# Fetches of the second pass held to set times, new planner durations, and one weight pair converted beside the last chunk's value products

## The chip, the cores and the metric

The kernel runs on one core of one Trainium2 chip. A core has TensorE (PE: matmuls, and their weight loads, shown as PEld), VectorE (DVE), ScalarE (ACT), GpSimd (POOL) and SyncE (SP), which here only issues DMAs. The metric is the device time of one execution in microseconds (us), lower is better.

## The reference

Three layers follow each other on a batch of 4 sequences of 576 tokens and 512 features, all in fp32. Attention is windowed: heads 0 to 3 look at the last 32 tokens, heads 4 to 7 at every fourth of the last 128.

```python
scores = scale * q @ k.T                      # masked per head to its window
x = softmax(scores) @ v                       # -> [4, 576, 512]

x_prev = shift of x by one token
xk = mu_k * x + (1 - mu_k) * x_prev
xr = mu_r * x + (1 - mu_r) * x_prev
k = maximum(xk @ w_k, 0)                      # 512 -> 1024
x = sigmoid(xr @ w_r) * (k * k @ w_v)         # 1024 -> 512

h = maximum(x.T @ w_tok1, 0) @ w_tok2         # over the tokens: 576 -> 256 -> 576
u = x + h.T
h2 = maximum(u @ w_ch1, 0) @ w_ch2            # 512 -> 1536 -> 512
out = u + h2
```

## The kernel before

**Arithmetic.** A product of fp32 values is made of three matmuls on split operands: each operand is kept as a high and a low part (two fp32r values), and high*high, high*low and low*high are added in PSUM. So each weight and each activation has to be converted first: ACT usually makes the high part (a copy with rounding) and DVE the low part (a subtraction). The two large channel products (`w_ch1`, `w_ch2`) go by a scheme with seven products of half blocks in place of eight, named A11, S1, A12, S2, S4, S3 and A22; for it, sums and differences of blocks of weights and activations are formed on DVE as well.

**Stages.** In the order of the program:

- attention, 36 units; the later ones lie beside the second layer;
- the second layer, in chunks of columns: `keys` (products with `w_k`), `mix` (products with `w_v`, here "value products"; they gather in the PSUM banks 68 to 70, and DVE frees a bank with a multiplication, `x<-x,bank`, before the next chunk's value products can use it) and `receptance` (products with `w_r`). The loop over `g` holds chunks 0 to 3, and the last chunk, chunk 5, comes behind it in a loop over `n` (`mixes(5, n)`);
- the third layer over tokens (a loop over `b`, the four sequences), then the first channel product, then the second one. The second channel product is called the second pass here: `result(c)` for c = 0, 1, 2, each for a third of the tokens.

**Weights converted early.** The weights of the channel products are converted while the second layer runs. `weight_1(j)` does pair j of column blocks of `w_ch1`: it loads two blocks, forms four sums, splits seven blocks into high and low parts and writes them to DRAM (`part_w`). `weight_ks(j)` makes sums of `w_k` blocks (`part_k`), `weight_2(j)` does a pair of `w_ch2` (`part_A`, `part_S`). The tables `W1_AT`, `K_AT` and `W2_LATE` say at which step g, or how early in the token stage, each one stands. They work in the tiles `raw`, `wv` and `x` (or, with the places called `amid`, in `xt` and `wk`).

**The second pass.** The first channel product's outputs are kept in DRAM (`part_mid`, three arrays of 8 pieces of 128x1152, 576 KB each), and so is u (`part_u`). `result(c)` loads its pieces with `load(q)`, q = 0 to 3 being the four quarters (two pieces each), and its part of u in two DMAs. Then it goes through seven sweeps of 36 matmuls each, A11, S1, A12, S2, S4, S3, A22. Between the sweeps DVE adds u or a sum to what a sweep left in PSUM (`plus`, in the trace `z<-bank,...` and `y<-bank,...`) and `send` writes 128x384 pieces of 192 KB to the output (`outT<-z`, `outT<-y`). The pieces to be sent lie in a ring of three places of two pieces each (`two(out_r)`: tiles named z, z and y), so that an addition into a place has to wait until that place's send before has landed. The sweep A22 goes on in the banks of S3, so that it can start only when DVE has read those banks.

**Order.** All instructions are first recorded by the class `Plan`, with the engines that may run each. `Plan.order` then plays the program with a duration for each instruction (`_cost`) and sets the order on each engine: of what is ready, the instruction with the earliest due time goes next. Due times come from the place of the TensorE work that needs a result. `hold` keeps an instruction from starting before its place in the program (the sum of TensorE time ahead of it) plus a number of us; `floor` makes conversions that were recorded through `slowly` due no earlier than 20 us behind their place, and sets their hold to 0; `SPARE` is time added behind a load that a conversion needs. Nothing of this is done on the chip: what is left there is one fixed order per engine, with semaphores between them. All instructions are issued from one line (L421), so the profile's groups are told apart by tile.

Of the kernel before, what the change touches and what calls it, by code (L numbers as in the profile page):

```python
# [19 lines left out]
C = H * D  # L20
# [33 lines left out]
TILES = [sum(n for _, _, n in c) // 128 for c in CHUNKS]  # L54
FIRST = [sum(TILES[:c]) for c in range(len(CHUNKS))]
N2 = 384
W1_AT, K_AT, W2_LATE, SLACK = (8, 11, 13, 16, 18, 21), (9, 12, 16, 19), (4, 7, 10, 13), 20.0
NAMES = "A11", "S1", "A12", "S2", "S4", "S3", "A22"
NEG = -1.0e30
MASKED = 1  # L60
# [94 lines left out]
class Plan:  # L155
# [17 lines left out]
    }  # L173
    TAIL = dict(tensor=0.0, vector=0.08, scalar=0.10, gpsimd=0.0, sync=0.0)
    TICK, BUSY = 10.24 / 3, 3060
    SPARE = 3.0

    def __init__(self, nc):
        self.nc = nc
# [77 lines left out]
    @staticmethod  # L257
    def _cost(engine, method, kw):

        out = kw["out"]  # L260
        cols = int(np.prod(out.shape[1:]))
        pointers = sum(hasattr(kw.get(k), "space") for k in ("scale", "bias", "scalar", "scalar1"))
        if engine == "sync":
            if kw["in_"].dtype == U32:
                return max(0.45, 4 * cols * out.shape[0] / 230e3 - 0.9)
            return max(0.45, 8 * (0.03 + 4 * cols * 0.0266e-3))
        if engine == "tensor":
            if kw.get("is_transpose"):
                return cols / 1200 + 0.0025
            if kw["lhsT"].dtype in (F32R, BF16):  # L270
                return cols / 2263 + 0.0049
            if kw["lhsT"].shape[0] <= D or out.shape[0] <= D:
                return cols / 1200 + 0.0025
            return 2 * max(cols / 1200 + 0.0025, 0.112)
        source = kw.get("in_", kw.get("in0"))
        psum = source is not None and "PSUM" in str(source.space)
        if engine == "scalar":
            read = 0.093 * (kw.get("accum_out") is not None)
            return (0.07 if psum else 0.1) + cols / 1200 + 0.03 * pointers + read
        if engine == "gpsimd":  # L280
            return 0.04 if method == "memset" else 0.04 + cols / 345
        if method == "tensor_reduce":
            return 0.066 + int(np.prod(source.shape[1:])) / 960
        if method == "reciprocal":
            return 0.066 + cols / 157
        fast = method in ("tensor_copy", "tensor_scalar", "tensor_scalar_add") and not psum
        return 0.066 + 0.05 * pointers + cols / (1920 if fast else 960)

    def _run(self, at, cost, kw):

# [144 lines left out]
def tile_model(nc, banks, kept_k, kept_1, kept_w, kept_u, kept_mid, units, cst, mu, w_k, w_v, w_r, w_t1, w_t2, w_c1, w_c2, outT):  # L435
# [21 lines left out]
    def ring(*places):  # L457
        return Ring(at, sum((p if isinstance(p, list) else [p] for p in places), []))
# [47 lines left out]
    def col_block(w, m, n=128):  # L506

        return words(w).rearrange("(k p) c -> p k c", p=128)[:, :, 2 * n * m:2 * n * m + 2 * n]
# [290 lines left out]
    def quarters(j, load, order, raws, fresh, both=both, sums=sums):  # L799

        for i in range(2):
            single([(everything, load(j + 6 * i))], both[:, i].flat(), raws)
        a11, a12, a21, a22 = (both[:, k // 2, k % 2] for k in order)
        combine(sums[:, 0], a21, a22, ALU.add)
        combine(sums[:, 1], sums[:, 0], a11, ALU.subtract)
        combine(sums[:, 2], a11, a21, ALU.subtract)
        combine(sums[:, 3], a12, sums[:, 1], ALU.subtract)
        for name, v in zip(NAMES, (a11, sums[:, 0], a12, sums[:, 1], sums[:, 3], sums[:, 2], a22)):
            t = fresh.tile(2, 256, dtype=F32R)
            split(v, t[:, 0], t[:, 1])  # L810
            yield name, f(t)

    def weight_1(j):
        for n, (_, t) in enumerate(quarters(j, lambda m: col_block(w_c1, m), (0, 1, 2, 3), raw_c, fresh)):
            nc.sync.dma_start(out=kept_1[j][:, n], in_=t)

    def weight_ks(j):
# [18 lines left out]
    def slowly(convert, *args):  # L836
        start = len(nc.ops)
        convert(*args)
        nc.floor.update(dict.fromkeys(range(start, len(nc.ops)), SLACK))
        nc.hold.update(dict.fromkeys(range(start, len(nc.ops)), 0.0))  # L840
# [3 lines left out]
    for g in range(8 * nchunk + 2):  # L844
        c, m = divmod(g, 8)
        kr = 2 if c else 0
        if g == 0:
            k_ring = psum(3)
        elif g == 10:
            k_ring, s_ring = psum(3, 4), psum(0)  # L850
        if m == 0 and c < nchunk:
            for which in range(2):
                for kt in KT:
                    prep(c, which, kt)
        if g >= 2:
            cv, mv = divmod(g - 2, 8)
            if cv == 0 and mv % 2 == 0:
                weight_v(mv // 2)
            for j in range(TILES[cv]):
                mix(cv, mv, j)  # L860
        if c == 0 and m % 2 == 0:
            weight_k(m // 2)
        if c < nchunk:
            keys(c, m, k_ring)
        if g in W1_AT:
            slowly(weight_1, W1_AT.index(g))
        if g in K_AT:
            slowly(weight_ks, K_AT.index(g))
        for h in beside.get(2 * g, []):
            attend(h, s_ring, t_ring, x_ring)  # L870
        if c < nchunk and kr <= m < kr + TILES[c]:
            if c == 0 and m == kr:
                for kt in range(4):
                    weight_r(kt)
            receptance(c, m - kr, k_ring)
        for h in beside.get(2 * g + 1, []):
            attend(h, s_ring, t_ring, x_ring)
# [95 lines left out]
    def mixes(c, n, first=5):  # L973
        m = order_m[n]
        h, l = (k2_r.tile(N2, dtype=F32R) for _ in range(2))
        split(k2[c, m], h, l)
        for j in range(TILES[c]):
            if n == 0:
                vp[j] = bank(first + j, (C,))
            mm3(vp[j], h[:, rows(j)], l[:, rows(j)], *wv[m], n == 0, n == 7)  # L980
            if n == 7:
                t = x2[FIRST[c] + j]
                nc.vector.scalar_tensor_tensor(out=t, in0=t, scalar=1.0, in1=vp[j], op0=ALU.add, op1=ALU.mult)
# [22 lines left out]
    receptance(4, 1, k_ring)  # L1006
    receptance(4, 2, k_ring)
    mixes(4, 7)
    for n in range(8):
        mixes(5, n)  # L1010
        if n % 2 == 0 and n < 6:
            receptance(5, n // 2, k_ring)

# [157 lines left out]
            r = rest[:, kt, 64 * (b % 2):64 * (b % 2) + 64].split(2, 32)  # L1171
            nc.vector.tensor_tensor(out=t, in0=r, in1=t, op=ALU.add)

    amid = ring(cut("xt", (2,), 2 * C)), ring(cut("wk", (2,), 512)), at(("wk", 3, 0), (2, 2, 256)), at(("wk", 3, 1024), (4, 256))
    for b in range(B):
        if b < 6 - len(W2_LATE):
            slowly(weight_2, b, *amid)
        tokens_in(b)
        if b == 2:
            for j in (1, 2):  # L1180
                fetch_1(j)
        if b:
            tokens_out(b - 1)
# [92 lines left out]
    def result(c):  # L1276
# [43 lines left out]

        x, y, z = two(x_r), two(y_r), two(z_r)
        on = dict(first=False, goes_on=True)
        load(0)
        load(1)
        for kt in range(4):
            nc.sync.dma_start(out=us[kt], in_=kept_u[c][:, kt])
        load(2)
        load(3)
        sweep("A11", parts(0), x)
        s1 = two(aside_r)  # L1330
        plus(x, u_of(0, 0), s1)
# [117 lines left out]
```

## Time and profile before

| | |
|---|---|
| device time, median of 3 runs | 673.16 us (673.02 to 673.44) |
| the profiled execution | 671.81 us |
| its span in the trace | 670.0 us |
| PE busy | 653.8 us, 98% |
| DVE, ACT, POOL busy | 566.7 (85%), 371.4 (55%), 2.1 us |
| TensorE's granted clock | 1.00 throughout (the 2.4 GHz level) |
| moved by DMA | 146.45 MB |

The profiled execution took 1.81 us more than its span, and was 1.35 us shorter than the median of the runs. Busy time is the share in which an engine executes; an engine's idle time is put down to whatever released it.

### The profile page before, as it was taken

What the parts mean: (1) busy time and instruction counts of PE and PEld (TensorE: products, weight loads), DVE (VectorE), ACT (ScalarE), POOL (GpSimd) and SP (SyncE); (2) the same over time, 40 slices, a digit from 0 to 9 for tenths busy, and PEclk for the clock granted to TensorE, in tenths of its full rate; (3) what the DMA queues carried; (4) which work ended last, traced back from release to release, by engine and by line L of the source; (5) the groups of instructions that cost most, each with busy time, mean ns of one, the idle gap of its engine ahead of it and who ended that gap; (6) DMA issues with size and microseconds to landing.
All of it is one profiled execution on the core that took longest, in us unless ns stands there. A gap on an engine that the chain in (4) does not pass through costs nothing.

```text
span 670.0 us, 11558 instructions
## 1 busy us (share of the span) xinstructions
PE 653.8 (98%) x4105; PEld 603.0 (90%) x4105; DVE 566.7 (85%) x1188; ACT 371.4 (55%) x981; POOL 2.1 (0%) x22
## 2 busy tenths in 40 slices
PE   6899999999999999999999999999999999899997
PEld 6678888888888888998889899999999999899997
DVE  4999998799799989777699888798898569899982
ACT  4989785789669875435278555264474122312310
POOL 0000000000000000000000000000000000000000
PEclk9999999999999999999999999999999999999999
DMA  8989444675774535713533769777697999933211
GB/s 325 385 310 331 142 126 150 190 261 166 249 237 149 198 115 179 237 38 121 164 111 133 233 193 364 275 254 256 247 356 253 413 408 412 392 107 95 71 36 59
DMA packets 65385, 146.45 MB, mean 219 GB/s; under 512 B 5808, under 2 KB 24368, under 8 KB 64304
## 3 DMA queue, kind: packets, MB, share of 16 engines
q1 hardware_dynamic: 65328, 145.72, 62.3%
q8 instruction: 32, 0.52, 0.3%
q14 instruction: 25, 0.20, 0.1%
HBM read 95.89 MB, written 49.81 MB: 217 GB/s over the span
## 4 chain that ended last, share of the span: by engine, by line
PE 72%; DVE 11%; DMA 9%; ACT 5%; issue 1%; SPq 0%; DVEq 0%; ACTq 0%
PE bank L421 72%; DVE z L421 3%; DVE at L421 2%; DVE x L421 2%; DMA z<-part_mid 2%; ACT z L421 2%; DVE wv L421 1%; ACT at L421 1%; ACT x L421 1%; DMA outT<-z 1%; DMA outT<-y 1%; DMA x<-w_k 1%; DMA wr<-units 1%; DMA part_mid<-at 1%; DMA at<-units 1%
## 5 line engine op out<-in xcount | busy, mean ns | idle before, releaser
L421 PE MATMUL bank<-z,wk 128*128 128x384 f32 x644 | 141.9, 345 | 0.3 <-ACT z L421 0.3
L421 PE MATMUL bank<-wv,z 128*128 128x512 f32 x432 | 124.3, 402 | 1.3 <-ACT raw L421 1.3
L421 PEld LDWEIGHTS bank<-z,wk 128*128 128x128 f32 x644 | 112.7, 188 | 5.7 <-ACT z L421 0.9
L421 PEld LDWEIGHTS bank<-wv,z 128*128 128x128 f32 x432 | 78.0, 188 | 14.6 <-ACT raw L421 1.6
L421 ACT ACTIVATE at<-at 128x96 f32<-128x96 f32 (+3 forms) x183 | 67.0, 369 | 36.3 <-DVE at L421 34.9
L421 ACT ACTIVATE z<-z 128x384 fp32r<-128x384 f32 (+1 forms) x90 | 46.4, 523 | 23.2 <-DVE z L421 15.7
L421 PE MATMUL bank<-xt,wk 128*128 128x384 f32 x254 | 54.0, 346 | 0.8 <-ACT at L421 0.8
L421 PE MATMUL bank<-wr,z 128*128 128x512 f32 x192 | 53.7, 406 | 1.0 <-DVE z L421 1.0
L421 PE MATMUL bank<-xt,x 128*128 128x384 f32 x248 | 48.8, 334 | 0.0
L421 PE MATMUL bank<-z,x 128*128 128x384 f32 x232 | 47.0, 334 | 0.0
L421 PEld LDWEIGHTS bank<-xt,wk 128*128 128x128 f32 x254 | 44.4, 188 | 2.6 <-issue 1.1
L421 DVE TENSOR_TENSOR z<-z,z 128x384 fp32r<-128x384 f32 (+1 forms) x78 | 44.2, 574 | 1.8 <-ACT z L421 0.6
L421 PEld LDWEIGHTS bank<-xt,x 128*128 128x128 f32 x248 | 43.5, 188 | 0.0
L421 DVE TENSOR_TENSOR at<-bank,at 128x384 f32<-128x384 f32 x64 | 35.2, 552 | 7.8 <-PE bank L421 7.2
L421 PEld LDWEIGHTS bank<-wr,z 128*128 128x128 f32 x192 | 34.3, 188 | 7.3 <-DVE z L421 1.3
L421 PEld LDWEIGHTS bank<-z,x 128*128 128x128 f32 x232 | 40.8, 188 | 0.0
L421 ACT ACTIVATE x<-bank 96x512 f32<-96x512 f32 (+1 forms) x48 | 28.1, 589 | 11.8 <-PE bank L421 11.6
L421 ACT ACTIVATE at<-bank 128x384 f32<-128x384 f32 x36 | 17.5, 488 | 27.0 <-PE bank L421 26.2
L421 DVE TENSOR_TENSOR raw<-raw 128x256 f32<-128x256 f32 (+1 forms) x76 | 30.2, 420 | 0.2
L421 PE MATMUL bank<-at 128*128 128x96 f32 (+1 forms) x121 | 22.1, 275 | 5.4 <-DMA at<-cst 5.0
L421 PE MATMUL bank<-cst,at 128*96 128x128 f32 x144 | 26.8, 274 | 0.2 <-DVE at L421 0.2
L421 PE MATMUL bank<-z,at 128*128 128x512 f32 x96 | 25.5, 397 | 0.0
(234 smaller groups left out, 1327.1 us busy)
## 6 DMA issues: line engine op xcount, KB each, us to landing
part_mid<-at SPq DMA_DIRECT2D x18, 768.0 KB, 5.9
z<-part_mid SPq DMA_DIRECT2D x11, 576.0 KB, 9.3
x<-w_c SPq DMA_DIRECT2D x12, 512.0 KB, 4.0
at<-units SPq DMA_DIRECT2D x14, 416.0 KB, 3.7
unit<-units SPq DMA_DIRECT2D x13, 416.0 KB, 3.8
at<-units SPq DMA_DIRECT2D x21, 256.0 KB, 3.4
part_w<-wv SPq DMA_DIRECT2D x21, 256.0 KB, 2.7
part_w<-x SPq DMA_DIRECT2D x21, 256.0 KB, 3.0
```

The costliest lines, as they stand in the source:

```text
L421: call(kw["out"], kw["constant"]) if method == "memset" else call(**kw)
```

## The change

- In `result(c)` the loads have the same order in the program as before (quarters 0 and 1, then u, then quarters 2 and 3), but for c = 1 and 2 each group now has a hold: -5, -5, 0, +5, +5 us against its place. Before they had none.
- In `_cost` the durations that the planner assumes for DMAs, ACT and DVE become longer; `SPARE` becomes 2 instead of 3.
- `W1_AT` has five steps instead of six. The sixth pair of `w_ch1` is now recorded in the last chunk, behind `mixes(5, 2)`, in the places `amid`.
- `weight_2(0)` is recorded behind `mixes(5, 5)` (before: at sequence 0 of the token stage), `weight_2(1)` at sequence 2 (before: at sequence 1). `K_AT` has later steps.

The number of instructions of each kind stays: what is computed is the same.

```diff
-W1_AT, K_AT, W2_LATE, SLACK = (8, 11, 13, 16, 18, 21), (9, 12, 16, 19), (4, 7, 10, 13), 20.0
+W1_AT, K_AT, W2_LATE, SLACK = (8,12,16,19,22), (10,14,18,21), (4,7,10,13), 20.0
...
-    SPARE = 3.0
+    SPARE = 2.0
...
-            return max(0.45, 8 * (0.03 + 4 * cols * 0.0266e-3))
+            return max(0.45, 8 * (0.045 + 4 * cols * 0.0266e-3))
...
-            return (0.07 if psum else 0.1) + cols / 1200 + 0.03 * pointers + read
+            return (0.08 if psum else 0.11) + cols / 1170 + 0.03 * pointers + read
...
-        return 0.066 + 0.05 * pointers + cols / (1920 if fast else 960)
+        return 0.075 + 0.05 * pointers + cols / (1860 if fast else 930)
...
+    amid = ring(cut("xt", (2,), 2 * C)), ring(cut("wk", (2,), 512)), at(("wk", 3, 0), (2, 2, 256)), at(("wk", 3, 1024), (4, 256))
     for n in range(8):
         mixes(5, n)
+        if n in (2,5):
+            slowly(*{2:(weight_1,5,*amid),5:(weight_2,0,*amid)}[n])
...
-        if b < 6 - len(W2_LATE):
-            slowly(weight_2, b, *amid)
+        if b in (2,):
+            slowly(*{2:(weight_2,1,*amid)}[b])
...
-        load(0)
-        load(1)
-        for kt in range(4):
-            nc.sync.dma_start(out=us[kt], in_=kept_u[c][:, kt])
-        load(2)
-        load(3)
+        for wait, first, q in ((-5.0, 0, 0), (-5.0, 0, 1), (0.0, 1, 0), (5.0, 0, 2), (5.0, 0, 3)):
+            start = len(nc.ops)
+            if first:
+                for kt in range(4):
+                    nc.sync.dma_start(out=us[kt], in_=kept_u[c][:, kt])
+            else:
+                load(q)
+            if c:
+                nc.hold.update(dict.fromkeys(range(start, len(nc.ops)), wait))
```

**SP around the end of `result(0)`.** SP issues the DMAs in this order where the sweeps S4, S3 and A22 of c = 0 run. `part_S` and `part_A` are the weights of the second pass, `part_mid_88` and `part_u_85` what c = 1 loads, `part_mid_89` what c = 2 loads. One more load of `part_mid_88` stands two rows ahead of this piece, at row 272. Before:

```order
274 L421 DMA wr_3_5442<-part_A_83 128x1024
275 L421 DMA z_2_5438<-part_mid_88 128x1152
276 L421 DMA z_2_5461<-part_mid_88 128x1152
277 L421 DMA at_2_4135<-part_mid_88 128x1152
278 L421 DMA outT<-z_2_5461 128x384
279 L421 DMA at_2_4184<-part_mid_88 128x1152
280 L421 DMA outT<-z_2_5438 128x384
281 L421 DMA at_2_4184<-part_mid_88 128x1152
282 L421 DMA wv_2_3622<-part_mid_88 128x1152 x2
283 L421 DMA unit_2_4088<-part_u_85 128x768
284 L421 DMA unit_2_4108<-part_u_85 128x768
285 L421 DMA outT<-y_4_5530 128x384
```

And in the changed kernel:

```order
276 L421 DMA wr_3_5434<-part_A_83 128x1024
277 L421 DMA wr_3_5446<-part_A_83 128x1024
278 L421 DMA outT<-z_2_5440 128x384
279 L421 DMA outT<-z_2_5461 128x384
280 L421 DMA z_1_5481<-part_mid_88 128x1152
281 L421 DMA z_2_5440<-part_mid_88 128x1152
282 L421 DMA z_2_5461<-part_mid_88 128x1152
283 L421 DMA at_2_4134<-part_mid_88 128x1152
284 L421 DMA unit_2_4088<-part_u_85 128x768
285 L421 DMA unit_2_4108<-part_u_85 128x768
286 L421 DMA outT<-y_4_5526 128x384
287 L421 DMA at_2_4186<-part_mid_88 128x1152 x2
```

Before, four loads of c = 1 stand ahead of the first of these sends, and eight and the two of u ahead of the send of y. Now none stands ahead of the first two sends, and four and the two of u stand ahead of the send of y.

**DVE where chunk 2's value products take over the banks.** `raw`, `wv_1` and `x_1` are tiles of the weight conversions, `at` and `z` belong to attention and to the chunk's own operands, and `x<-x,bank_68` frees a bank of the value products. Before:

```order
312 L421 TENSOR_TENSOR x_1_1229<-raw_0_320,x_1_1229 128x256
313 L421 TENSOR_TENSOR at_0_142<-bank_63,at_0_114 128x384
314 L421 TENSOR_TENSOR raw_0_320<-wk_0_715 128x512
315 L421 TENSOR_REDUCE at_0_142<-at_0_142 128x4
316 L421 TENSOR_TENSOR raw_0_320<-raw_0_320 128x256 x3
317 L421 TENSOR_TENSOR wv_1_831<-raw_0_320,wv_1_831 128x256
318 L421 TENSOR_TENSOR raw_0_320<-raw_0_320 128x256
319 L421 TENSOR_TENSOR x_1_1229<-raw_0_320,x_1_1229 128x256
320 L421 SCALAR_TENSOR_TENSOR x_0_727<-x_0_727,bank_68 128x512
```

And in the changed kernel:

```order
326 L421 TENSOR_TENSOR at_0_140<-at_0_140 128x384
327 L421 TENSOR_TENSOR raw_0_345<-wk_0_717 128x512
328 L421 SCALAR_TENSOR_TENSOR z_0_351<-xt_0_101,cst_0_111,z_0_351 128x256
329 L421 TENSOR_TENSOR raw_0_345<-raw_0_345 128x256
330 L421 TENSOR_TENSOR at_0_140<-bank_63,at_0_114 128x384
331 L421 SCALAR_TENSOR_TENSOR z_0_351<-xt_0_96,cst_0_111,z_0_351 128x64
332 L421 TENSOR_REDUCE at_0_140<-at_0_140 128x4
333 L421 SCALAR_TENSOR_TENSOR x_0_731<-x_0_731,bank_68 128x512
```

Seven conversion instructions stood among the last eight ahead of the first freed bank (the row with x3 counts three), now two among the last seven.

**DVE at the end of chunk 5, changed kernel.** Here `wk_2` and `wk_0` are the tiles of the early conversions (`amid`), `raw` and `at` belong to the token stage's weights, and `x<-x,bank` frees a bank of the last value products; rows between are left out, as their numbers show.

```order
636 L421 TENSOR_TENSOR wk_2_3270<-wk_2_3270 128x256 x3
646 L421 TENSOR_TENSOR wk_0_717<-wk_2_3270,wk_0_717 128x256
651 L421 TENSOR_SCALAR wk_2_3270<-wk_2_3270 128x512
653 L421 SCALAR_TENSOR_TENSOR wk_2_3270<-xt_0_106,wk_2_3270 128x512
657 L421 TENSOR_TENSOR wk_0_717<-wk_2_3270,wk_0_717 128x256
660 L421 TENSOR_TENSOR wk_0_717<-wk_2_3270,wk_0_717 128x256
675 L421 SCALAR_TENSOR_TENSOR x_2_3317<-x_2_3317,bank_68 128x512
676 L421 SCALAR_TENSOR_TENSOR x_0_188<-x_0_188,bank_69 128x512
678 L421 SCALAR_TENSOR_TENSOR x_0_188<-x_0_188,bank_70 128x512
679 L421 TENSOR_TENSOR wk_0_717<-wk_2_3270,wk_0_717 128x256
```

The added pair has 15 instructions on DVE (two shifts, two SCALAR_TENSOR_TENSOR of 128x512, four sums and seven low parts of 128x256). The last low parts are at rows 657 and 660, so the pair stands whole ahead of the freed banks; from row 651 on `weight_2(0)` begins, which stood in the same region before.

## Rows read from the trace of the kernel before

**Rows 1.** Page, busy time: engine, busy us, share, instructions.

```profile
PE 653.8 (98%) x4105; PEld 603.0 (90%) x4105; DVE 566.7 (85%) x1188; ACT 371.4 (55%) x981; POOL 2.1 (0%) x22
```

**Rows 2.** PE's waits, whole run: waited for, us in total, times, longest.

```profile
PE bank L421 <- DMA at<-cst: 5.0, 1, 5.0
PE bank L421 <- issue: 1.9, 1, 1.9
PE bank L421 <- ACT raw L421: 1.3, 1, 1.3
```

**Rows 3.** Busy time by stretch: us, PE, PEld, DVE, ACT, POOL, clock, DMA share, GB/s.

```profile
310.00:341.00 31.00, 31.00 (x139) 25.65 (x138) 20.32 (x49) 12.46 (x26) 0.00 (x0) 1.00 0.37 115
341.00:381.00 40.00, 40.00 (x233) 35.39 (x232) 39.63 (x106) 29.34 (x72) 0.00 (x0) 1.00 0.45 150
520.00:570.00 50.00, 50.00 (x290) 49.95 (x289) 36.01 (x45) 11.04 (x12) 0.00 (x0) 1.00 1.03 411
570.00:580.00 10.00, 7.94 (x44) 7.38 (x43) 7.38 (x9) 3.16 (x3) 0.00 (x0) 1.00 1.03 415
```

**Rows 4.** Chain that ended last, second pass: start, us, what.

```profile
557.95 8.51 DMA outT<-z
566.52 8.50 DMA outT<-y
```

**Rows 5.** PE's timeline, S3 and A22 of c = 0: start, us, [idle before].

```profile
563.86 6.41 PE L421 MATMUL bank<-wv,x 128*128 128x384 f32 x36
572.21 6.93 PE L421 MATMUL bank<-xt,wr 128*128 128x384 f32 x36 [1.94 <-issue]
```

**Rows 6.** DVE's timeline there, the three additions into sent places.

```profile
568.43 0.56 DVE L421 TENSOR_TENSOR z<-bank,z 128x384 f32<-128x384 f32 x1 [1.18 <-DMA outT<-z]
...
571.56 0.55 DVE L421 TENSOR_TENSOR z<-bank,z 128x384 f32<-128x384 f32 x1
...
575.11 0.56 DVE L421 TENSOR_TENSOR y<-bank,z 128x384 f32<-128x384 f32 x1 [0.94 <-DMA outT<-y]
```

**Rows 7.** SP's timeline there (issues).

```profile
564.55 1.75 SPq L421 DMA_DIRECT2D unit<-part_u  x2
566.52 0.34 SPq L421 DMA_DIRECT2D outT<-y  x1
```

**Rows 8.** DMAs issued 520 to 600: KB, median us to landing; then all `outT`.

```profile
z<-part_mid SPq DMA_DIRECT2D x11, 576.0 KB, 9.3
...
outT<-z SPq DMA_DIRECT2D x6, 192.0 KB, 8.5
...
unit<-part_u SPq DMA_DIRECT2D x2, 384.0 KB, 8.7
...
DMA to landing us min/median/max: 1.8/1.9/9.3
```

**Rows 9.** DVE's and PE's timelines where chunk 2's value products begin.

```profile
158.26 0.68 DVE L421 TENSOR_TENSOR raw<-wk 128x512 f32<-128x512 f32 x1
...
159.32 1.09 DVE L421 TENSOR_TENSOR raw<-raw 128x256 f32<-128x256 f32 x3
...
161.33 0.43 DVE L421 TENSOR_TENSOR x<-raw,x 128x256 fp32r<-128x256 f32 x1
161.67 0.68 DVE L421 SCALAR_TENSOR_TENSOR x<-x,bank 128x512 f32<-128x512 f32 x1
...
162.50 0.71 PE L421 MATMUL bank<-wv,z 128*128 128x512 f32 x2 [1.27 <-ACT raw L421]
```

**Rows 10.** PE's timeline in the attention at the start.

```profile
24.71 0.69 PE L421 MATMUL bank<-x,wr 96*64 96x64 f32 x16 [0.80 <-DVE xt L421]
...
26.72 1.53 PE L421 MATMUL bank<-xt,wk 128*128 128x384 f32 x4 [0.75 <-ACT at L421]
```

**Rows 11.** DVE's timeline in the token stage.

```profile
384.24 0.46 DVE L421 COPY wv<-bank 128x288 f32<-128x288 f32 x1 [1.88 <-PE bank L421]
386.30 0.46 DVE L421 COPY wv<-bank 128x288 f32<-128x288 f32 x1 [1.59 <-PE bank L421]
```

More of the change, by code (lines that the diff above doesn't have):

```diff
@@ L811, in quarters, with weight_1 @@
             yield name, f(t)
-    def weight_1(j):
-        for n, (_, t) in enumerate(quarters(j, lambda m: col_block(w_c1, m), (0, 1, 2, 3), raw_c, fresh)):
+    def weight_1(j, *places):
+        for n, (_, t) in enumerate(quarters(j, lambda m: col_block(w_c1, m), (0, 1, 2, 3), *places)):
             nc.sync.dma_start(out=kept_1[j][:, n], in_=t)
@@ L865, in tile_model @@
         if g in W1_AT:
-            slowly(weight_1, W1_AT.index(g))
+            slowly(weight_1, W1_AT.index(g), raw_c, fresh)
         if g in K_AT:
@@ L1172, in tokens_out @@
             nc.vector.tensor_tensor(out=t, in0=r, in1=t, op=ALU.add)
-    amid = ring(cut("xt", (2,), 2 * C)), ring(cut("wk", (2,), 512)), at(("wk", 3, 0), (2, 2, 256)), at(("wk", 3, 1024), (4, 256))
     for b in range(B):
-        if b < 6 - len(W2_LATE):
-            slowly(weight_2, b, *amid)
+        if b in (2,):
+            slowly(*{2:(weight_2,1,*amid)}[b])
         tokens_in(b)
```

## The prediction

> **What bounds the kernel now.** I read the page's busy times first: PE executes for 653.8 of the span's 670.0 us [rows 1]. So no more than 16.2 us can be won as long as TensorE's work stays the same, and the change leaves it the same; what counts is only what makes PE wait. The table of PE's waits comes next [rows 2]. The largest, 5.0 us, is the first load, which the change doesn't touch. The two that follow are one wait of 1.9 us put down to "issue", and one of 1.3 us put down to ACT's tile raw. The timelines give their places. The 1.9 us stand before the sweep A22 of c = 0, at 572.21 [rows 5]; the 1.3 us are at 162.50, where the value products of chunk 2 want the banks of chunk 1 [rows 9]. Of the smaller ones, two lie at 24.71 and 26.72, 1.55 us together [rows 10].
>
> "Issue" names no cause, so I followed A22 back. It goes on in the banks that S3 left, so DVE must have read both. DVE's reads are the additions `z<-bank,z` at 568.43 and 571.56; the second ends at 572.11 and PE starts 0.10 us later [rows 5, 6]. The first had waited 1.18 us for a send `outT<-z` to land [rows 6], which the chain of waits shows as well: that send took 8.51 us from its issue, and the send of y behind it 8.50 [rows 4]. Over the whole run the median send takes 1.9 us [rows 8]. What lengthens these is the traffic: from 520 to 580 the DMA share is 1.03, and 411 to 415 GB/s move [rows 3]. The sends stand behind loads in that stream. So a part of the kernel in which PE is otherwise full waits for a 192 KB write of a tile, not for any data that it multiplies.
>
> **The second pass, step by step.** The set times move sends ahead of loads. In the order before, four loads of `part_mid` for c = 1 are issued ahead of the first send, and eight and two of u ahead of the send of y; after the change none, and four and two. At 411 GB/s a load of 576 KB takes 1.43 us, one of u (384 KB) 0.96, a send 0.48, a weight piece of 512 KB 1.28 (bytes from [rows 8] and the widths in the order, rate from [rows 3]).
>
> First send: at its issue time of before, 557.95 [rows 4], at most the six weight pieces that stand in front of it are under way, 7.7 us if none had landed. Then the two sends land by 566.6 at the latest, and not before 557.95 + 1.9 = 559.9 [rows 4, 8]; I take the middle, 563. DVE could start its addition at 568.43 - 1.18 = 567.25 [rows 6]. So the whole 1.18 us goes away, by either bound. The second addition, and with it A22, moves up by as much: PE's wait falls from 1.94 to about 0.76, because what is late next is DVE's own work between the two additions.
>
> Send of y: A22 is interrupted once more. Its 36 matmuls take 6.93 us where S3's 36 take 6.41 [rows 5], 0.5 more, while the addition `y<-bank,z` at 575.11 waited 0.94 us for the send of y [rows 6]. That send was issued at 566.52, behind the two loads of u [rows 7]. In the new order it has four loads, two of u and itself behind the first sends: 4 x 1.43 + 2 x 0.96 + 0.48 = 8.1 us. From 563 that is 571.1, from the worst 566.6 it is 574.7. DVE will want it at 575.11 - 0.94 - 1.18 = 572.99. I take the first, so this 0.5 us goes as well: **-1.7 us** in all. Bounds: -1.2 where the send of y stays late, -2.4 (1.94 + 0.5) where both stalls vanish.
>
> The loads that now come later feed c = 1 and 2, from the sweep that follows A22 at 578.98 or so. What is pushed back is four loads of `part_mid_88` and those of `part_mid_89`, which c = 2 needs a third of the pass later. I cost that at nothing, by the cover of the seven sweeps of c = 1 (7 x 6.4 us, [rows 5]); without that cover a late load would cost up to its own 9.3 us [rows 8].
>
> A rule of the Trainium skill speaks against this step. DMA: Bandwidth & Descriptors, section "Queues, rings and completion order", says that data descriptors carry no barrier, so that a later DMA may finish before an earlier one: completion is not first in, first out. By that rule the place of a send among the loads would settle little, and the sum of this part would be 0. The trace shows sends that took 8.5 us in the full stream, about what the loads around them took (8.7 and 9.3), against 1.9 outside it [rows 8]: the short writes did not overtake. So I keep -1.7.
>
> **The first pass.** The wait of 1.27 us at 162.50 is put down to ACT, yet the ACT instruction that ends there only copies weights. What PE needs is a free bank, and DVE frees one in `x<-x,bank` from 161.67 to 162.35 [rows 9]. In front of it DVE ran seven conversion instructions of the early weights: one of 0.68, three in 1.09, and three of some 0.43 [rows 9], 3.1 us together. In the new order two conversions are left among the seven rows ahead, some 1.1 us. The freed bank could come up to 2.0 us earlier by that, more than the wait; but the attention rows between them must be ready too, and these depend on ACT and PE. I take 0.9 of 1.27. Bounds: all of it, or nothing, or a wait of the same size that appears at another boundary since all conversions were shifted (+1.3).
>
> **The moved pair.** It leaves the region of chunks 0 to 3, in which PE waits for hardly anything but the above, so its removal there gives nothing more. In chunk 5 it adds 15 DVE instructions of about 0.43 us, an estimate of 6.5 us from the row at 161.33 [rows 9]. DVE has 31.0 - 20.3 = 10.7 us to spare from 310 to 341 [rows 3], and the new order has the pair whole ahead of the last freed banks. Cost: 0. Without that cover it falls into 341 to 381, where DVE is busy 39.6 of 40 us [rows 3], and is late by 6.5 us, less the 1.88 + 1.59 us that DVE waits for PE at 384 and 386 [rows 11].
>
> **The new durations.** They move the start too: the conversion of `w_k` comes behind more attention work. Of the two waits there, 1.55 us [rows 10], all could go; or the products with `w_k` come late by a wait of like size, 0.8. I take 0. The trace gives no row for what a whole new order costs elsewhere.
>
> Sum: -1.7 - 0.9 = -2.6 us. Against the profiled execution, 671.81, that makes 669.2; against the median of the runs, which is 1.35 us higher, **670.5 us**. A measurement of this kernel can tell some 0.2% (1.35 us) from no change: faster means under 671.8, slower over 674.5.
>
> **Rivals.**
>
> - Only the second pass gains, and the first pass finds its waits elsewhere: 673.2 - 1.7 = 671.5, between 671 and 672.5. For it: PE's waits are short and scattered, and a new order makes new ones.
> - The sends stay late: the DMA stream is full by 1.03 whatever its order, and the weights in front of the sends may land later, since the loads and the writes of the last converted pair are shifted too. Then the first-pass gain alone is left, 672.3, or nothing, 673.2. The cited rule would lead here as well. Against it: the two bounds above, and rows of 8.5 us.
> - More: both stalls of the second pass (-2.4), all of 1.27 and the 1.55 at the start: 673.2 - 5.2 = 668.0.
> - Slower: chunk 5's pair isn't ready ahead of the freed banks, as its two loads or ACT's high parts come late, and DVE, which works in order, holds the last `x<-x,bank` behind it. The price is up to 6.5 us; with the second pass's 1.7 won, it passes 674.5 when over 3.1 us of the pair are left uncovered, and reaches 673.2 + 6.5 - 1.7 = 678.0 if all are. Against it: 10.7 us to spare on DVE and 18.5 on ACT from 310 to 341 [rows 3].
>
> **How the numbers follow.** The forecast (669.3 to 671.3): 0.45. Only the second pass: 0.20, of which I put a half below 671.8. More than forecast, 667.5 to 669.3: 0.10. Sends late or all of it lost again: 0.13. Slower: 0.12, of which 0.10 over 674.5. Faster is 0.45 + 0.10 + 0.10 + 0.02 = 0.67, slower 0.10, the same 0.23. The range from 668.0 to 673.6 leaves out about 0.12 above and 0.05 below.
>
> **What would show it.** In the changed profile, the additions `z<-bank,z` of c = 0 should show no wait for `outT<-z` near 567, the wait before A22 should be 0.8 us or less and A22's sweep near 6.4; the chain should not go through `outT`. PE should wait under 0.5 us where chunk 2's value products begin. From 310 to 341 DVE should be about 6.5 us busier, with PE's busy share still 1.00 up to 381. The prediction fails if sends near 558 still take over 8 us, if a load of `part_mid` or u becomes what c = 1 waits for, or if PE shows new waits of over a microsecond before 400.

## The result, and the profile after

The changed kernel takes 663.86 us (median of 4 runs, 663.56 to 664.65) against 673.25 us before (673.02 to 673.44): a ratio of 0.9862 with a 95% interval of 0.9845 to 0.9880. That is 9.4 us less, where 2.6 were forecast. A second set of runs of the same kernel gave 663.66 us, ratio 0.9862 (0.9844 to 0.9880).

The profiled execution took 663.9 us, with a span of 662.1. The page's busy times, and the table of PE's waits, which answer to [rows 1] and [rows 2]:

```profile
PE 650.5 (98%) x4105; PEld 602.3 (91%) x4105; DVE 562.0 (85%) x1174; ACT 383.4 (58%) x995; POOL 2.1 (0%) x22
```

```profile
PE bank L421 <- DMA at<-cst: 5.5, 1, 5.5
PE bank L421 <- issue: 0.8, 1, 0.8
PE bank L421 <- DVE z L421: 0.6, 1, 0.6
PE bank L421 <- DVE at L421: 0.5, 1, 0.5
PE bank L421 <- ACT z L421: 0.3, 1, 0.3
```

Both of the waits on which the forecast rested are gone from the table; the `issue` row that is left is another wait, of 0.82 us at 24.78 in the attention. But the span is 7.9 us shorter, and only 4.6 of these are time in which PE stood idle (16.2 us before, 11.6 now): PE's busy time fell by 3.3 us too, with the same 4105 matmuls. In this trace a matmul's end is modelled, so a matmul that starts a little late, or runs at a lower clock, counts as busy. So the busy time of before held stalls that no row of the waits shows.

The second pass, by the timelines of PE and DVE around the end of c = 0, which answer to [rows 5] and [rows 6], and a line on the transfers that answers to [rows 8]:

```profile
558.49 6.41 PE L421 MATMUL bank<-wv,x 128*128 128x384 f32 x36
564.75 6.49 PE L421 MATMUL bank<-xt,wr 128*128 128x384 f32 x36
```

```profile
560.98 0.55 DVE L421 TENSOR_TENSOR z<-bank,z 128x384 f32<-128x384 f32 x1
...
564.10 0.55 DVE L421 TENSOR_TENSOR z<-bank,z 128x384 f32<-128x384 f32 x1
...
566.65 0.56 DVE L421 TENSOR_TENSOR y<-bank,z 128x384 f32<-128x384 f32 x1
```

```profile
outT<-z SPq DMA_DIRECT2D x6, 192.0 KB, 7.4
```

S3 and A22 now follow each other without a gap, A22 takes 6.49 us instead of 6.93, and none of the three additions waits. The sends still take 7.4 us to land, since the stream is as full as before; they are only issued early enough. The chain of waits between 500 and 600 is now a single piece:

```profile
499.89 100.12 PE bank L421 x577
```

In the first pass the first freed bank of chunk 1, at 161.67 in [rows 9], comes at 155.78:

```profile
155.78 0.67 DVE L421 SCALAR_TENSOR_TENSOR x<-x,bank 128x512 f32<-128x512 f32 x1
```

Windows that answer to [rows 3] show the moved pair: from 310 to 341 DVE is busy 28.48 us instead of 20.32, and PE still all of the time.

```profile
310.00:341.00 31.00, 31.00 (x138) 25.69 (x137) 28.48 (x68) 17.65 (x38) 0.00 (x0) 1.00 0.50 165
341.00:381.00 40.00, 40.00 (x236) 35.39 (x236) 36.64 (x97) 28.56 (x72) 0.00 (x0) 1.00 0.58 193
```

### The profile page after: what moved, and what is told of

Same layout as the page of the kernel before. It is cut to its first block, busy times and chain, and to the rows that moved or that the text cites. A ratio compares the mean times of both kernels' runs of the same rounds, so it can differ in the third digit from the quotient of the medians.

```text
span 662.1 us, 11564 instructions
## 1 busy us (share of the span) xinstructions
PE 650.5 (98%) x4105; PEld 602.3 (91%) x4105; DVE 562.0 (85%) x1174; ACT 383.4 (58%) x995; POOL 2.1 (0%) x22
## 4 chain that ended last, share of the span: by engine, by line
PE 92%; DVE 3%; ACT 2%; DMA 1%; issue 0%; SPq 0%; ACTq 0%
PE bank L421 92%; DVE at L421 2%; DMA raw<-w_v 1%; ACT x L421 1%; DMA at<-cst 1%; DVE x L421 1%; ACT at L421 1%; ACT z L421 0%; ACT xt L421 0%; DVE wv L421 0%; DVE z L421 0%; DVE wr L421 0%; DVE unit L421 0%; SPq L421 0%; ACT wk L421 0%
## 5 line engine op out<-in xcount | busy, mean ns | idle before, releaser
L421 PE MATMUL bank<-wv,z 128*128 128x512 f32 x432 | 126.7, 404 | 0.0
L421 ACT ACTIVATE z<-z 128x384 fp32r<-128x384 f32 (+1 forms) x102 | 52.3, 521 | 25.1 <-DVE z L421 22.1
L421 DVE TENSOR_TENSOR raw<-raw 128x256 f32<-128x256 f32 (+1 forms) x72 | 28.8, 420 | 0.2
L421 PE MATMUL bank<-wv,x 128*128 128x384 f32 x132 | 24.8, 334 | 0.0
```

The source lines that it names most:

```text
L421: call(kw["out"], kw["constant"]) if method == "memset" else call(**kw)
```

## Where the time went, for all runs

Since the order of the matmuls differs, I compared the executions by work done: each matmul start is weighted with its usual interval to the next (0.173 us for 384 columns, 0.227 for 512, and so on), these are added in order, and the table gives how much later (+) or earlier (-) than in the first profile of before the same sum is reached. The head is the time of that point in that profile. All values are us.

```
                60.0  149.9  169.7  303.3  567.0  584.7
before_again   +0.08  +0.39  +0.37  +0.32  -0.25  +1.15
after          -1.11  -2.04  -3.78  -4.66  -5.38  -7.90
after_again    -1.03  -1.37  -3.11  -3.98  -4.65  -7.03
holds_only     +0.14  +0.22  +0.22  +0.20  -0.12  -1.60
no_holds       -1.75  -2.68  -4.41  -5.29  -5.97  -2.13
costs_only     +0.66  -0.26  -1.92  -2.78  -3.16  -0.89
no_costs       +0.06  -0.27  -1.80  -2.71  -3.09  -4.66
tables_only    -0.07  -0.38  -1.91  -2.81  -3.19  -3.00
no_tables      -1.70  -2.61  -4.28  -5.16  -5.80  -7.34
late_write     +0.09  +0.15  +0.14  +0.12  -0.29  -1.75
sync_only      +0.50  +0.02  -1.03  -1.28  -1.44  +3.66
bank_first     +0.01  +0.00  -0.42  -0.52  -0.22  +3.10
hold_c1        -0.70  -1.61  -3.35  -4.25  -4.92  -5.95
```

With the median interval of each shape as weight, the columns 60.0 and 169.7 of the changed orders come out 0.3 us nearer to before, the others the same. Behind the last column nothing changes in any of them. So there are five places: the start, the stretch up to 150, the boundary at 162, the stretch from 256 to 303, and the end of c = 0 in the second pass (567 to 585). The changed kernel gains in all five.

## The experiments

### The four parts, alone and left out

**Set fetch times alone.** Before, with the loop over `wait` in `result(c)` and nothing else:

```diff
-        load(0)
-        load(1)
...
+        for wait, first, q in ((-5.0, 0, 0), (-5.0, 0, 1), (0.0, 1, 0), (5.0, 0, 2), (5.0, 0, 3)):
...
+                nc.hold.update(dict.fromkeys(range(start, len(nc.ops)), wait))
```

> Before, with the set fetch times of result(c) alone; the order up to the second pass stays that of before. Theory 1 (the sends waited behind loads): the stall at 572 goes, and the time falls by 1.7 as predicted up to the 2.5 us that the two profiles differ by between 552 and 585; 670.7 to 671.6. Theory 2 (the end of the second pass gained because what comes ahead of it was ordered anew): no change, 673.2, and the stall at 572 stays.

Measured: 670.21 us, ratio 0.9963 (0.9950 to 0.9977), so theory 1. DVE's and PE's timelines:

```profile
567.28 0.55 DVE L421 TENSOR_TENSOR z<-bank,z 128x384 f32<-128x384 f32 x1
...
570.41 0.55 DVE L421 TENSOR_TENSOR z<-bank,z 128x384 f32<-128x384 f32 x1
```

```profile
571.06 6.48 PE L421 MATMUL bank<-xt,wr 128*128 128x384 f32 x36 [0.91 <-issue]
```

This is the prediction's step to the letter: the first addition starts at 567.28 (567.25 worked out), 0.91 us of the wait are left (0.76), A22's own gap is gone. By the table the second pass gains 1.5 us against the first profile of before, whose clock stayed at 1.00. By the medians it is 2.8; the section on the clock has the difference.

**Everything but the set fetch times.** The changed kernel, with the loads of `result(c)` as before:

```diff
-            if c:
-                nc.hold.update(dict.fromkeys(range(start, len(nc.ops)), wait))
```

> The changed kernel without the set fetch times. Theory 1: it loses what the sends cost, 1.7 to 2.5 us, so 665.6 to 666.4. Theory 2: 663.9, no stall at the end of the second pass's first third.

Measured: 668.98 us, ratio 0.9941 (0.9926 to 0.9955). Without them the changed kernel is 5.1 us slower, twice what theory 1 gave. DVE's and PE's timelines, and a window over A22:

```profile
564.10 0.56 DVE L421 TENSOR_TENSOR z<-bank,z 128x384 f32<-128x384 f32 x1 [3.73 <-DMA outT<-z]
```

```profile
567.88 9.13 PE L421 MATMUL bank<-xt,wr 128*128 128x384 f32 x36 [3.59 <-issue]
```

```profile
567.90:577.00 9.10, 9.10 (x37) 9.10 (x38) 7.00 (x8) 1.84 (x2) 0.00 (x0) 0.68 1.03 417
```

Two things are to be seen. The execution reaches 567 with 6.0 us in hand (the table), and DVE is ready for its first addition 6.9 us earlier than before (560.37 against 567.25); but the send that it awaits lands only 4.3 us earlier, so the wait is 3.73 us instead of 1.18. And behind the wait of 3.59 us the granted clock is 0.68 on average over A22's 36 matmuls: they take 9.13 us instead of 6.4, with not one wait among them. So this stall costs itself and 2.7 us of lower clock. Of 6.0 us won ahead, 3.8 are lost here.

What made the send late can be read from SP, which issues in order. In this kernel the last write of a converted block, `part_S<-y`, is issued at 541.75, and the third load of `part_S` behind it has to wait until that write has landed. This holds SP for 3.4 us, with all that it issues later. In before the write goes out at 521.73 already and holds nothing. SP's waits and timeline of `no_holds`, then the timeline of before:

```profile
SPq L421 <- DMA part_S<-y: 3.4, 1, 3.4
```

```profile
541.75 0.43 SPq L421 DMA_DIRECT2D part_S<-y  x1
542.22 4.76 SPq L421 DMA_DIRECT2D x<-part_S  x3
```

```profile
521.73 0.81 SPq L421 DMA_DIRECT2D part_S<-y  x1
...
548.19 1.38 SPq L421 DMA_DIRECT2D x<-part_S  x3
```

The other kernels without set times divide the same way. Where the write goes out early, PE waits about 2 us before A22, however far ahead the execution is: 1.94 and 2.19 in the two profiles of before, 2.14 in `tables_only`, which is 3.2 us ahead. Where it goes out late, SP waits 3.4 to 4.5 us for it, and PE's wait is longer: 3.59 in `no_holds`, 3.2 in `costs_only`, 4.8 in `sync_only`, and 3.0 in `bank_first`, which is hardly ahead at all (0.22). So the longer stall goes with this write, and not with the time won ahead. That is read from the traces; no run moved the write alone without set times. The changed kernel has the same late write, but there no load of c = 1 stands ahead of the two sends, and they land in time.

**The planner's durations and `SPARE` alone, and the tables alone.** Before, with one of these two groups of lines (the tables with the moved pair and the moved `weight_2`):

```diff
+    SPARE = 2.0
...
+            return max(0.45, 8 * (0.045 + 4 * cols * 0.0266e-3))
...
+            return (0.08 if psum else 0.11) + cols / 1170 + 0.03 * pointers + read
...
+        return 0.075 + 0.05 * pointers + cols / (1860 if fast else 930)
```

```diff
+W1_AT, K_AT, W2_LATE, SLACK = (8,12,16,19,22), (10,14,18,21), (4,7,10,13), 20.0
```

> Before, with the planner's longer durations and SPARE 2 alone. Theory A (each part gains in its own places, and the parts add): the durations bring the 1.6 us of the first 60 us and part of the boundary at 162, so some 2.5 to 4 us less than before, 669.3 to 670.8. Theory B (the gain of the first 310 us belongs to one particular order that only both edits together give): between 672 and 674.

> Before, with the new tables and the pairs moved, the old durations and no holds. Theory A: the conversions that left chunks 2 and 3 give the 1.0 us between 256 and 305 and part of the boundary at 162: 1 to 2.7 us less than before, 670.5 to 672.3, and the start is as before. Theory B: between 672 and 675.

Measured: 668.89 us (0.9936, 0.9918 to 0.9953) and 669.61 us (0.9951, 0.9937 to 0.9966). Each won a little more than theory A gave it, but they don't add: together they are `no_holds`, 668.98. The table tells why. Both win the boundary at 162 (some 1.6 us) and the stretch from 256 (0.9), the same time by either way. And in the last column the kernels with the late write give back what they had won, 2.3 us in `costs_only` and 3.8 in `no_holds`, while `tables_only` gives back 0.2. At the start the tables bring nothing. The durations show no gain there in this execution, whose granted clock was low once early; the window from 40 to 50:

```profile
40.00:50.00 10.00, 9.84 (x45) 7.97 (x46) 9.06 (x19) 7.71 (x25) 0.10 (x1) 0.83 0.93 330
```

**The changed kernel without the durations, and without the tables.** The same two groups of lines, each undone in the changed kernel:

> The changed kernel with the old durations and SPARE 3 (set fetch times and new tables kept). By theory A the start loses its 1.6 us again, and the last weight write part_S_82 goes out early as in before, which leaves 0.9 us of the stall before A22; the boundary at 162 stays won: 663.9 + 2.5 = 666.4. Theory B (all of the first half's gain hangs on the pair of edits): 668 or more.

> The changed kernel with the old tables and pairs where they were (durations, SPARE and set fetch times kept). By theory A the durations alone give the start, the boundaries and the late write, and the tables add nothing to them: 663.5 to 664.5. Theory B: 666 or more.

Measured: 667.83 us (0.9923, 0.9905 to 0.9941) and 664.48 us (0.9874, 0.9856 to 0.9892). The first is 1.4 us above what theory A gave and just under the 668 of theory B; but by the table the boundary and the stretch from 256 stay won, which B excludes. Without the durations the start is that of before (+0.06 at 60 us), with them, and without the tables, it is 1.70 ahead: the start's gain is that of the durations and `SPARE`. And the tables, with the moved pair and all, can't be told from nothing once the durations are there: 664.48 against 663.86 and 663.66, with intervals that overlap. So theory B falls here too.

**The changed kernel again.**

> The changed kernel once more, beside these, for the difference to the same kernel with the old tables (664.48 there). If the tables and the moved pair add something to the durations and set times, it is 663.9 or less; if nothing, 664.2 to 664.8. The granted clock should be 1.00 in nearly all of its runs.

Measured: 663.66 us, as told. That lies in the range expected if the tables add something, and leaves them at some 0.8 us or nothing: `no_tables` has a wait of 0.82 us before A22, and neither profile of the changed kernel has it. In its profile the table is less far ahead at 150 (-1.37 against -2.04) than in the first: 0.5 us and more of the early places vary from one execution to the next.

### The clock in the kernel before

> The kernel before once more, for a second profile: the first profiled execution (671.81) was 1.4 us shorter than the median of its runs, and had the granted clock at 1.00, while most runs of before show 0.995 to 0.997 and those of the changed kernel 1.000. Theory C (the clock): where this execution has less than 1.00, the stretch of lower clock lies right behind the stall before A22 (568 to 576), and costs 1 to 2 us there; a time of 673. Rival: the longer runs lose the time elsewhere, in the loads at the start.

Measured: 672.96 us, with the clock at 0.997. PE's timeline and two windows, 572 to 580 and 580 to 585:

```profile
572.21 8.07 PE L421 MATMUL bank<-xt,wr 128*128 128x384 f32 x36 [2.19 <-issue]
```

```profile
572.00:580.00 8.00, 7.79 (x36) 7.82 (x37) 5.38 (x7) 2.07 (x2) 0.00 (x0) 0.79 1.03 418
580.00:585.00 5.00, 5.00 (x31) 5.00 (x30) 4.80 (x6) 1.17 (x1) 0.00 (x0) 1.00 1.05 382
```

The stall is 2.19 us here, and the granted clock falls behind it; A22 takes 8.07 us instead of 6.93. Up to 567 the two executions of before agree within 0.4 us, at 585 they are 1.4 apart (+1.15 from -0.25). That is what the first profile of before had not shown, and most of why it was 1.4 us under the median. Over the 54 runs of before that stand beside these experiments, 17 with a clock of 1.00 have a median of 672.2 us, 24 with 0.997 one of 673.1, 10 with 0.995 one of 674.1. The changed kernel's runs show 0.999 or 1.000.

### Single mechanisms

**The last weight write held back.** With the set times alone 0.9 us of the wait were left; in the changed kernel none. There the last write of a converted block goes out later. So this run has the set times, and in addition:

```diff
+                if 6 * c + j == W2_LATE[-1]:
+                    writes = [i for i in range(first, len(nc.ops)) if "sync" in nc.ops[i] and not isinstance(nc.ops[i]["sync"][1]["out"], View)]
+                    nc.hold[writes[5]] = 45.0
```

> Before with the set fetch times, and with the one write of a converted block part_S_82 held back by 45 us, so that it is issued behind the loads of part_mid for c = 0 instead of ahead of them. Theory D: with the set times alone 0.9 us of the stall before A22 are left since DVE's unbroken chain of work begins 4.4 to 4.7 us into S1's sweep, when z<-part_mid lands; in the three kernels that issue the write late it begins at 3.3 to 3.6. So the chain begins 0.8 us earlier, PE waits 0 to 0.2 before A22 and the time is 669.4 to 669.7, 0.5 to 0.9 less than with the set times alone. Rival: the late write does nothing, 670.2, and the remaining wait had to do with the different order on DVE.

Measured: 670.30 us (0.9956, 0.9940 to 0.9972), as with the set times alone, and 0.92 us of wait before A22. Theory D falls as it was put; and `no_tables`, which writes late too, keeps 0.82 us. The run is no clean test of the load: DVE got `z<-part_mid` at 542.38, 3.9 us into S1's sweep instead of 4.7 with the set times alone, but the planner gave DVE's next work another order, and one more wait stands in it.

```profile
542.38 1.36 DVE L421 TENSOR_TENSOR wv<-z,wv 128x1152 f32<-128x1152 f32 x1 [5.28 <-DMA z<-part_mid]
...
551.67 0.56 DVE L421 TENSOR_TENSOR z<-bank,at 128x384 f32<-128x384 f32 x1 [0.54 <-DMA at<-part_u]
```

Where the last 0.8 us of this wait lie can be read from DVE. In `holds_only`, `no_costs`, `no_tables` and the changed kernel it works without a gap from a conversion that had waited for `z<-part_mid` up to the second addition, which starts 27.0 us behind that conversion in all four. The conversion starts 4.6 to 4.7 us into S1's sweep in the first three, and 3.6 us into it in the changed kernel. DVE's and PE's timelines of `no_tables`, then of the changed kernel:

```profile
537.64 0.76 DVE L421 CAST wv<-z 128x1152 fp32r<-128x1152 f32 x1 [6.64 <-DMA z<-part_mid]
```

```profile
533.07 7.96 PE L421 MATMUL bank<-xt,wk 128*128 128x384 f32 x45
```

```profile
537.11 0.76 DVE L421 CAST wv<-z 128x1152 fp32r<-128x1152 f32 x1 [5.36 <-DMA z<-part_mid]
```

```profile
533.53 7.96 PE L421 MATMUL bank<-xt,wk 128*128 128x384 f32 x45
```

So the load lands 1 us sooner there against PE's work, and the wait is gone. Theory D had this chain right, and only its cause wrong; what brings the load sooner in the changed kernel stays open.

**The freed bank first.** Before, with one line more in `mix`, for chunk 1 alone:

```diff
+            if c == 1:
+                nc.early[len(nc.ops) - 1] = 14.0
```

> Before, with one thing more: the three multiplications that free the value banks of chunk 1 get due times 14 us earlier, so DVE runs the first one five rows (six conversions and one reduction, 2.8 us) sooner; the order on DVE up to there is that of before. Theory F (PE's wait at 162.50 is DVE's queue of conversions ahead of the freed bank, not ACT as the profile names it): the wait falls from 1.27 to under 0.2, and behind it the execution is 1.2 to 1.7 us ahead; total 671.5 to 672. Rival (ACT's copy, or the attention's own chain, holds PE): the wait stays over 1 us and the total at 673.

Measured: 673.27 us (1.0008, 0.9995 to 1.0021), no change. DVE's row of the freed bank and the PE row that now waits:

```profile
158.86 0.68 DVE L421 SCALAR_TENSOR_TENSOR x<-x,bank 128x512 f32<-128x512 f32 x1
```

```profile
165.09 0.96 PE L421 MATMUL bank<-wv,z 128*128 128x512 f32 x3 [0.85 <-DVE z L421]
```

Theory F is half right. The bank is free 2.81 us sooner, as worked out, and the wait at 162.50 is gone, so it was DVE's queue and not ACT: PE goes on with the value products at 162.47, while the copy on ACT that the profile of before had named ends at 163.11 here. But 2.6 us later PE waits 0.85 us for the operands that DVE had put behind: the conversions were still to be done. At 169.7 only 0.42 us are left, and the second pass takes that and more: its stall is 3.0 us, with the sends behind loads as in before and the write `part_S<-y` issued late. Putting DVE's work in another order moves its backlog; the changed kernel, and each of the two parts alone, has less backlog there.

**The DMA durations alone.** Before, with one line:

```diff
-            return max(0.45, 8 * (0.03 + 4 * cols * 0.0266e-3))
+            return max(0.45, 8 * (0.045 + 4 * cols * 0.0266e-3))
```

> Before, with the longer DMA durations of the planner alone (0.045 for 0.03). They put the conversion of w_k on DVE and ACT behind the bank copies of the attention at the start, as in the changed kernel; at the boundary at 162 ten conversions still stand in the twelve rows ahead of the freed bank, and the sends stand behind one to five loads of part_mid. Theory E (at the start, ACT and DVE waited in order behind a load of w_k that the planner thought sooner): PE's waits at 24.7 and 26.7 go, and at 60 us the execution is 1.0 to 1.7 us ahead of before; the wait at 162 stays (1 us or more). Rival: the start needs the longer ACT and DVE durations, and is within 0.4 us of before. The total lies in both cases near 671 to 673, so the place decides.

Measured: 674.97 us (1.0032, 1.0019 to 1.0045), slower than before. Theory E falls: the wait at 26.7 is gone, the one at 24.7 is not, and at 60 us it is 0.50 behind. The wait at 162, which was expected to stay at 1 us or more, shrank to 0.29 us, though ten conversions still stand in the rows ahead of the freed bank.

```profile
25.39 0.69 PE L421 MATMUL bank<-x,wr 96*64 96x64 f32 x16 [0.80 <-DVE xt L421]
...
161.66 0.47 PE L421 MATMUL bank<-wv,z 128*128 128x512 f32 x1 [0.29 <-ACT x L421]
```

The start needs the ACT and DVE durations as well; which of them does it was not taken apart. The total is worse by the second pass: it arrives 1.4 us ahead, and stalls for 4.8 us, with the late write ahead of the sends and a lower clock behind.

**Set times for c = 1 alone.** A dose: one 576 KB load of c = 2 comes between the first two sends.

```diff
-            if c:
+            if c == 1:
```

> The changed kernel with the set times for c = 1 alone; the loads of c = 2 are free again. Against the changed kernel, one load of part_mid_89 (576 KB) is issued between the first two sends, and the rest stand between the later ones; nothing ahead of them changes. Theory 1, as a dose: a load ahead of a send makes it land 1.4 us later. The first addition isn't held (its send stands first, and the second one had 2.5 us to spare), so there is no wait before A22; the send of y lands 1.4 us later, which DVE has no room for, so y<-bank waits 1 to 1.5 us and A22 takes up to 0.9 us longer; 663.7 to 664.8. Rival (the c = 2 loads matter as much as those of c = 1, since all share the queue): a wait of 1 us or more before A22 and 665.5 or more.

Measured: 664.85 us (0.9874, 0.9857 to 0.9892), and a wait of 1.36 us before A22, which I had not expected. The time lies between what theory 1 gave (up to 664.8) and what the rival gave (665.5 or more); the wait is the rival's. DVE's timeline, between the first and the second addition:

```profile
563.13 1.36 DVE L421 TENSOR_TENSOR xt<-z,xt 128x1152 fp32r<-128x1152 f32 x1 [0.96 <-ACT xt L421]
564.78 1.36 DVE L421 TENSOR_TENSOR z<-z,z 128x1152 f32<-128x1152 f32 x1 [0.29 <-DMA z<-part_mid]
566.06 0.55 DVE L421 TENSOR_TENSOR z<-bank,z 128x384 f32<-128x384 f32 x1
```

No send is awaited, so they did have room. But the loads of c = 1, behind one more transfer of 1.4 us, feed two conversions that stand on DVE ahead of the second addition; the first of them waits for ACT, which waits for such a load as well. So as a dose for the sends the run decides little. The set times need both sides: loads behind the sends of c = 0, and no later than DVE's next rows want them.

## Why the prediction was wrong

Against the usual execution of before (`before_again`) and by the table's differences, the changed kernel wins 1.2 us at the start, 1.2 up to 150, 1.7 at the boundary, 0.8 from there to 303, 0.2 to 567 and 3.9 in the second pass: 9.0 in all. By the steps of the prediction:

- **The second pass, -1.7.** The mechanism, sends that stand behind loads, was right, and `holds_only` shows it. The step that failed is the size: 3.9 us were won. The sum was made against one profiled execution, whose clock was 1.00 throughout; most executions lose more behind the stall by a lower clock (1.4 us in `before_again`, 0.9 by the medians of the runs with 1.00 and 0.997). And in the changed kernel the remaining 0.76 us go too. In the new order the set times are worth 5.1 us, since without them the late write would hold the loads and sends behind it; the rival "the sends stay late" had that write in view, but the sends now stand ahead of the loads of c = 1 and land in time.
- **The send that was awaited.** One reading was wrong, and it changed nothing in the sum. The first addition did not wait for the send of 8.51 us in [rows 4], but for the second one, issued at 559.01 behind one load more, which took 9.3 us. The chain names the first because SP waited for its landing before it issued the send of y. In before, of the send issued at 559.01 alone:

```profile
L421 SPq DMA_DIRECT2D outT<-z x1: 338/338/338, 559.0 to 559.0; - x1
...
  DVE z L421: 1.2, 1
...
DMA to landing us min/median/max: 9.3/9.3/9.3
```

- **The rule of the Trainium skill** (DMA: Bandwidth & Descriptors, "Queues, rings and completion order"). That completion isn't first in, first out was not seen here: in every run the sends landed behind the loads issued ahead of them, and putting them ahead is what won.
- **The boundary, -0.9 of 1.27.** The wait is gone and the place won 1.7. The reading that DVE and not ACT held PE is shown by `bank_first`; that the number of conversions in the rows ahead decides is not: with these moved behind, most of the wait came back 2.6 us later, and in `sync_only` the wait shrank to 0.29 us with ten of them still ahead. DVE's backlog over the whole stretch fits both, but no run took it apart.
- **The start, 0 (bounds -1.55 and +0.8).** It won 1.1 to 1.7. I had both waits in view and took 0 between the bounds, with no row for it: a term that was left at nothing. Of their 1.55 us 0.82 are left; a wait of 0.96 us at 50.92, which the prediction did not list, went as well, and one of 0.62 at 37.76 came. The row that I had named, `w_k`'s conversion behind the attention's copies, is not the cause by itself: `sync_only` has it there and wins nothing. By the runs of the parts the gain belongs to the durations and `SPARE`; which of them brings it stays open.
- **No gain elsewhere in chunks 0 to 3.** This is the step that failed outright: "PE waits for hardly anything but the above". From 256 to 303 and up to 150 another 2 us were won (1.5 in the second profile of the changed kernel), where the table of waits shows PE waiting for next to nothing: one row of 0.39 us at 146.85, for the attention's work on DVE. The chain of waits would have told. From 60 to 150 its only long piece on PE in before is the one from 99.55 to 136.16, while in the changed kernel it is on PE all of the time. Around 275 in before it leaves PE for DVE from 275.36 to 277.49, with no idle time of PE in between; in the changed kernel it stays on PE from 252 to 320:

```profile
275.36 0.04 DVE z L421
275.40 0.44 issue
275.84 1.13 DVE at L421 x3
276.97 0.48 DVE z L421
277.45 0.04 issue
277.49 2.67 PE bank L421 x13
```

```profile
251.98 68.16 PE bank L421 x338
```

  And the first pass up to 170, in before and in the changed kernel:

```profile
99.55 36.61 PE bank L421 x240
```

```profile
50.63 119.56 PE bank L421 x897
```

  The whole run's chain of before had it as well, as a row "DVE at" at 275.84 between two long ones of PE. What in the new order keeps DVE ahead of PE at these places was not taken apart: the durations alone and the tables alone both win the stretch from 256.
- **The moved pair, 0.** Right: 8.2 us more of DVE work from 310 to 341 (6.5 estimated for the pair alone; the window also holds the start of `weight_2(0)`), PE not held. The tables as a whole gave at most some 0.8 us on top of the durations.
- **Rivals.** "More" gave 668.0 at the most, with a chance of 0.10. It lacked the clock and the hidden stalls. The 16.2 us outside PE's busy time were taken for all that could be won, but 3.3 of the 7.9 us came out of the busy time.

## What to carry to other kernels

Before a stall is priced, compare the profiled execution's granted clock and time with the other runs: one that is shorter than the median may be the one in which the stall did no further harm. Ahead of a stretch that leans on one full DMA queue, look at what holds that queue's issues: time won earlier was kept where the queue moved along (`tables_only`), and in part lost where a load had to wait for a late write (`no_holds`, 3.8 of 6.0 us). Here the early gains alone were worth 4 us and the place of the sends alone 3, and both together 9.4. And a change to a planner's durations is judged by place, with the same work lined up in both traces, since single waits move rather than vanish.

## What the runs showed of the hardware

A stall of TensorE of 1.94 us left the granted clock at 1.00 in one execution, and so did one of 2.14 us in `tables_only`; one of 2.19 us in the kernel before was followed by a stretch with a mean of 0.79, and one of 3.59 us by A22's matmuls at a mean of 0.68, between the two levels of 1.2 and 2.4 GHz; 36 matmuls then took 8.07 and 9.13 us instead of 6.4. No wait appears in the table for that time.

All 355 transfers that SP issued landed in the order of their issue, in each of the 14 profiles. A send of 192 KB took 1.9 us in the median over the kernel before, and 9.3 us behind loads of 576 KB at 411 GB/s.
